# Side-by-side key-value products for batch 0 of an attention and highway kernel, and a new order of its steps

## The chip, the core and the metric

The kernel runs on one core of a Trainium2 chip. A core has five engines that run side by side, each through its own queue and in the order of that queue: TensorE (PE in the profile, with PEld for its weight loads), VectorE (DVE), ScalarE (ACT), GpSimd (POOL) and SyncE (SP), which here only issues DMAs. Engines wait for each other by semaphores. TensorE writes to PSUM; VectorE and ScalarE read it, GpSimd works on SBUF alone. The metric is the device time of one execution in microseconds.

## The reference

Eight batches, eight heads, 576 positions, 64 values a head. First an attention without a score matrix, then a highway layer:

```python
q_s = exp(q);  q_s = q_s / sum(q_s, over the head's 64 values)
k_s = exp(k);  k_s = k_s / sum(k_s, over the 576 positions)
kv  = einsum('bhsd,bhse->bhde', k_s, v)           # 64 x 64 for each batch and head
x   = einsum('bhsd,bhde->bhse', q_s, kv)          # then (4608, 512): all heads of a position in a row
H   = maximum(x @ w_h, 0)
T   = sigmoid(x @ w_t + b_t)
out = T * H + (1 - T) * x
```

Inputs and output are float32 in the chip's main memory: q, k and v 9.4 MB each, the output 9.4 MB.

## The kernel before, in words

Positions are put on partitions: 64 rows of 9 positions, for two heads at once, so that a [128, 4, 9 x 64] tile holds a batch (4 pairs of heads, called chunks). The work is cut into 36 tiles of 128 positions, nine for each pair of batches (tile 8, 17, ... holds the ninth positions of both batches). All of it is written as short steps with names, and the string `ORDER` (lines 16 to 63) lists some 710 of them. A loop at the end (lines 502 to 505) runs through that list and issues each step's instructions. Nothing is rescheduled, so the list sets the order of every engine's queue, and of SP's DMA queue too. A name has a batch or tile and a part; a letter behind a colon picks the engine (A ScalarE, D VectorE, P GpSimd, F a whole step at once).

The steps, in the order in which one tile needs them:

- `k`, `v`, `q`, `w`: loads of the inputs and the two weights (SP). `st`: stores of the output (SP). A tile of q, k or v has three buffers. Batches 0 to 2 load k and v in pieces (`load_kv`, line 181).
- `ek`: exp of k on ScalarE (line 252). `vc`: cast of v to half precision on any engine (258), into a tile that has a column of ones behind each 64 values.
- `kv`: for each position j, head of a pair and row half, one matmul of ek (stationary) with v and its ones (264), so that 65 columns hold kv and the sum of the exponentials. The accumulator `ps` has a PSUM bank for each row half. Batches 0 to 2 do it in two steps, chunks 0 and 1 (`kv_b_0`: k and v chunks 0, 1) and chunks 2 and 3 (`kv_b_1`); the others in one. `kr` takes the reciprocal of the sums (280) and `kn` multiplies with it into `kvb` (285), both on VectorE.
- `eq`: exp of q on ScalarE (295). `qt`: its transposes on TensorE (313). `qc`: their copy to SBUF (331). For batch 7 a DMA transposes (`qd`, 339).
- `xu`: q times kv and, by a column of ones, q's sum (350). `rs`, `x`: the division, on VectorE (369, 374). `xt`: transposes of x (381). `xe`: their copy (389), on VectorE or ScalarE.
- `bw`: the bias of the gate into its accumulator (396), by a ScalarE copy or a matmul; the gate has two banks. `mt`: the gate's four products (408). `mh`: those of the other branch (416).
- `th`: tanh in place of the sigmoid (430). `dd`: the maximum, on VectorE (439). `uu`: (tanh + 1) times it, on VectorE in one instruction or, with P, on GpSimd in two (443). `oo`: plus x (464).
- `whd`, `whc`, `wtc`: the weights' adjustment (the identity is taken from w_h) and cast. `bp`, `bc`, `bsplit`: the bias spread over 128 rows. `fill_n`: n matmuls of a blank tile into a spare bank (166), whose results nobody reads.

Some tiles (0, 4, 5, 6, 7) do xu to mh in two halves, each with one part of the heads; the last tile does its gate in two pieces of columns.

Of the kernel before, what the change touches and what calls it, by code (L numbers as in the profile page):

```python
# [26 lines left out]
xe_4_0:D xe_4_1:D mh_5_0 dd_5 mt_5_0 th_5_0 uu_5_0:P k_2_0 ek_2_1 bw_8:A ek_2_2 xu_6_0 rs_6_0 x_6_0 mt_4_1 xt_8_0
xe_8_0:D xu_6_1 rs_6_1 qt_2_0 x_6_1 xu_7_0 rs_7_0 x_7_0 mt_4_0 xt_6_0 xu_7_1 rs_7_1 xt_6_1 xe_6_0:D xe_6_1:D x_7_1
mt_8_0 ek_2_0 v_2_0 vc_2_0:D qc_2_0 mh_4_1 mh_4_0 xt_7_0 dd_4 xt_7_1 th_4_0 vc_2_1 kv_2_0 v_2_2 vc_2_3 vc_2_2:A kv_2_1
kr_2_1 mh_8_0 bw_6:A mh_6_1 th_8_0 mt_6_1 kr_2_0 oo_5_0 kn_2_1 uu_4_0:P kn_2_0 xu_9_0 dd_8 q_2_4 eq_2_2 eq_2_1 xe_7_1  # L30
uu_8_0:P oo_4_0 rs_9_0 x_9_0 mt_6_0 xe_7_0 qt_2_1 qc_2_1 th_6_0 mh_6_0 dd_6 mh_7_1 xt_9_0 xu_12_0 rs_12_0 x_12_0
uu_6_0:P oo_8_0 oo_6_0 xe_9_0:D mh_7_0 dd_7 bw_7:A mt_7_1 mt_7_0 xu_10_0 xt_12_0 mh_9_0 xe_12_0:D rs_10_0 q_3_0 x_10_0
eq_3_0 eq_3_1 qt_3_2 qc_3_2 dd_9 mh_12_0 xt_10_0 xe_10_0:D qt_3_1 qc_3_1 k_3_0 th_7_0 bw_10:A v_3_0 vc_3_0 xu_11_0
rs_11_0 bw_9:A mt_9_0 ek_3_0 ek_3_2 dd_12 vc_3_2:A x_11_0 qt_3_0 th_9_0 qc_3_0 uu_7_0:P oo_7_0 uu_9_0 mt_10_0 th_10_0
bw_12:A kv_3_0 qt_2_2 q_4_0 qc_2_2:A mh_10_0 eq_4_0:F kr_3_0 kn_3_0 xt_11_0 xe_11_0:D mt_12_0 dd_10 uu_10_0:P oo_9_0
oo_10_0 xu_14_0 rs_14_0 x_14_0 th_12_0 uu_12_0 oo_12_0 mh_11_0 qt_4_0 bw_11:A xu_13_0 rs_13_0 x_13_0 v_4_0 vc_4_0
xt_14_0 xe_14_0:D vc_4_2:A bw_14:A mt_11_0 th_11_0 xu_17_0 rs_17_0 x_17_0 qc_4_0:A xt_13_0 mh_14_0 dd_11 uu_11_0:P
oo_11_0 xu_15_0 rs_15_0 xe_13_0:D x_15_0 mt_14_0 dd_14 mh_13_0 xu_16_0 rs_16_0 x_16_0 bw_13:A xt_17_0 xe_17_0:D
mt_13_0 dd_13 k_4_0 ek_4_0 ek_4_2 q_4_9 kv_4_0 kr_4_0 kn_4_0 th_14_0 uu_14_0:P bw_17:A th_13_0 uu_13_0 xt_15_0 xe_15_0
qt_4_1 qc_4_1 mt_17_0 xu_18_0 rs_18_0 x_18_0 oo_14_0 q_5_0 eq_5_0 oo_13_0 v_5_0 vc_5_0 bw_15:A vc_5_2 mh_17_0 xt_16_0  # L40
xe_16_0:D dd_17 eq_4_2 eq_5_1 mt_15_0 th_15_0 xu_20_0 qt_4_2 k_5_0 rs_20_0 x_20_0 mh_15_0 th_17_0 uu_17_0:P oo_17_0
xt_18_0 mh_16_0 xu_19_0 dd_15 qc_4_2 xe_18_0:D rs_19_0 qt_5_0 qc_5_0 bw_16:A ek_5_0:F xt_20_0 x_19_0 q_6_0 xe_20_0:D
mt_16_0 th_16_0 bw_18:A qt_5_1 kv_5_0 eq_6_0:F dd_16 kr_5_0 kn_5_0 uu_16_0 bw_20:A xt_19_0 mh_18_0 qc_5_1:A st_1_0
st_1_1 mh_20_0 st_3_0 uu_15_0:P oo_15_0 xe_19_0:D xu_21_0 rs_21_0 x_21_0 oo_16_0 mt_18_0 th_18_0 k_6_0 st_3_1 v_6_0
mt_20_0 xu_22_0 dd_18 uu_18_0 oo_18_0 st_5_0 st_7_1 q_5_9 st_5_1 xt_21_0 rs_22_0 x_22_0 th_20_0 dd_20 uu_20_0:P
xe_21_0:D st_7_0 qt_6_0 mh_19_0 xu_23_0 rs_23_0 x_23_0 vc_6_2 dd_19 bw_19:A bw_21:A mt_19_0 ek_6_0 ek_6_2 mh_21_0
dd_21 xt_22_0 xe_22_0 xu_24_0 mt_21_0 mh_22_0 xt_23_0 rs_24_0 qc_6_0 x_24_0 vc_6_0:A kv_6_0 qt_6_1 th_19_0 uu_19_0:P
oo_20_0 q_6_9 dd_22 xe_23_0:D mh_23_0 kr_6_0 th_21_0 uu_21_0 oo_19_0 kn_6_0 bw_22:A mt_22_0 qc_6_1:A dd_23 xu_25_0
rs_25_0 x_25_0 eq_5_2 xt_24_0 qt_5_2 bw_23:A mt_23_0 th_22_0 oo_21_0 uu_22_0:P oo_22_0 qc_5_2:A xu_26_0 xe_24_0
rs_26_0 x_26_0 bw_24:A th_23_0 uu_23_0 xt_25_0 mh_24_0 dd_24 st_10_1 q_7_0 oo_23_0 v_7_0 st_10_0 vc_7_0 vc_7_2 k_7_0  # L50
mt_24_0 xe_25_0 eq_6_2 xu_27_0 qt_6_2 xt_26_0 mh_25_0 rs_27_0 x_27_0 xe_26_0:D xu_29_0 rs_29_0 bw_25:A mt_25_0 st_17_0
eq_7_0:F qd_7_0 qc_6_2:A dd_25 th_24_0 qd_7_1 x_29_0 xt_27_0 xe_27_0 uu_24_0 oo_24_0 mh_26_0 dd_26 xu_30_0 rs_30_0
th_25_0 x_30_0 st_12_0 uu_25_0:P mh_27_0 bw_27:A mt_27_0 st_14_1 dd_27 xt_30_0 xu_28_0 rs_28_0 q_7_9 st_12_1 bw_26:A
mt_26_0 st_14_0 st_23_0 st_16_0 st_16_1 xe_30_0:D mh_30_0 ek_7_0 oo_25_0 x_28_0 xt_28_0 xe_28_0:D ek_7_2 kv_7_0
xt_29_0 th_26_0 uu_26_0 oo_26_0 th_27_0 uu_27_0:P mh_28_0 bw_30:A mt_30_0 kr_7_0 kn_7_0 xu_31_0 st_21_0 bw_28:A
mt_28_0 dd_30 xe_29_0:D rs_31_0 dd_28 th_30_0 uu_30_0:P mh_29_0 x_31_0 xt_31_0 xe_31_0:D oo_27_0 oo_30_0 bw_29:A
xu_33_0 eq_7_2 th_28_0 rs_33_0 uu_28_0 mt_29_0 qt_7_2 bw_31:A mh_31_0 x_33_0 xt_33_0 xu_32_0 th_29_0 dd_29 rs_32_0
uu_29_0 qc_7_2:A oo_29_0 x_32_0 xe_33_0 mt_31_0 mh_33_0 xt_32_0 bw_33:A th_31_0 dd_31 st_8_0 st_19_0 st_26_0 xu_34_0
xe_32_0 uu_31_0 rs_34_0 mt_33_0 x_34_0 oo_28_0 st_28_0 st_30_0 oo_31_0 st_31_0 st_25_0 mh_32_0 xu_35_0 dd_33 xt_34_0
bw_32:A mt_32_0 th_33_0 uu_33_0:P oo_33_0 dd_32 xe_34_0:D mh_34_0 rs_35_0 x_35_0 xt_35_0 bw_34:A th_32_0 uu_32_0 dd_34  # L60
xe_35_0 mt_34_0 th_34_0 uu_34_0 oo_32_0 st_33_0 st_32_0 oo_34_0 st_34_0 bw_35_0 mh_35_0 dd_35 mt_35_0 th_35_0 uu_35_0
# [5 lines left out]
def kernel(  # L67
# [49 lines left out]
    spare = turned.rearrange("p a c d -> p (a c d)").bitcast(FP32)
    T = {}
# [142 lines left out]
        copy(v16[b % NV][:, c:c + n, :, 0:D], T[f"v32{b}"][:, c:c + n].rearrange("p c (j d) -> p c j d", j=NJ))  # L261


    def kv(e, b, k):
        ps = once(f"kvps{b}", lambda: ps_x.tile([P, 2, DM], FP32, tag="xu", name=f"kv_{b}"))
        for kk in range(*halves(b, k)):
            for j in range(NJ):
                for hh in range(2):
                    for w in range(2):
                        rows, cols = slice(64 * hh, 64 * hh + 64), slice(64 * w, 64 * w + 64)  # L270
                        nc.tensor.matmul(  # L271
                            ps[cols, hh, 65 * kk:65 * kk + 65], T[f"ek{b}"][rows, j, 2 * kk + w],
                            v16[b % NV][rows, 2 * kk + w, j, 0:65],
                            start=(j == 0), stop=(j == NJ - 1), skip_group_check=True)
# [261 lines left out]
```

## Time and profile before

| | |
|---|---|
| median of 3 runs | 117.8 us (117.66 to 118.46) |
| the profiled execution | 117.78 us |
| its span | 116.0 us |
| TensorE busy | 109.2 us, 1355 matmuls |
| VectorE, ScalarE, GpSimd busy | 93.7, 91.2, 90.9 us |
| moved by DMA | 40.58 MB, mean 350 GB/s |
| mean granted TensorE clock | 0.99 |

The span reaches from the first to the last event that the profile has of the core; 1.78 us of the profiled execution lie outside it. A group of instructions goes by its line in the code. The slices cut the span into 40 parts of 2.9 us and give each engine's busy share in tenths. Matmul ends are modelled, so a busy TensorE is not always a TensorE at its peak. The chain is followed back from the last instruction, at each step to what released it. Times in the views count from the span's start.

### The profile page before, as it was taken

How to read it: one execution, taken by the hardware profiler on the slowest of the kernel's cores; microseconds unless marked ns; L12 is line 12 of the kernel's file. 1: busy time of each engine (PE TensorE's matmuls, PEld its weight loads, DVE VectorE, ACT ScalarE, POOL GpSimd, SP SyncE). 2: the span in 40 equal slices, each digit the busy share in tenths (PEclk: the TensorE clock that was granted, in tenths of full speed). 3: DMA queues.
4: the chain of work that ended last, by engine and by line, in shares of the span. 5: the costliest groups of instructions: out<-in, count | busy, mean ns of one | idle time of the engine just before them, and what ended most of it. 6: DMA issues, size and time to landing. Idle time of an engine off the chain costs nothing.

```text
span 116.0 us, 3454 instructions
## 1 busy us (share of the span) xinstructions
PE 109.2 (94%) x1355; PEld 62.8 (54%) x1355; DVE 93.7 (81%) x231; ACT 91.2 (79%) x139; POOL 90.9 (78%) x103
## 2 busy tenths in 40 slices
PE   5999999999999999999999999999999999999930
...
PEclk9999999999999999999999999999999999999995
DMA  2999999999999999999999999999999999894965
GB/s 49 375 397 379 407 391 378 390 377 367 384 384 379 390 393 366 367 393 355 349 386 388 363 401 406 391 384 332 370 398 376 148 276 394 343 364 166 401 257 181
DMA packets 24755, 40.58 MB, mean 350 GB/s; under 512 B 5410, under 2 KB 12834, under 8 KB 24740
## 3 DMA queue, kind: packets, MB, share of 16 engines
...
q10 hardware_dynamic: 148, 0.14, 0.4%
...
## 4 chain that ended last, share of the span: by engine, by line
PE 54%; POOL 26%; DVE 6%; issue 6%; DMA 2%; ACT 1%; POOLq 1%; ACTq 0%
POOL o L473 14%; PE gps L421 14%; PE tps L413 13%; PE turned L168 10%; POOL u L453 6%; PE kv L271 4%; PE xu L363 4%; PE turned L386 4%; PE qps L326 3%; POOL g L452 3%; DMA out_dram<-o 2%; POOL v L261 2%; DVE x L378 2%; DVE d L441 2%; DVE xT L393 1%
## 5 line engine op out<-in xcount | busy, mean ns | idle before, releaser
L473 POOL TENSOR_TENSOR o<-u,x 128x512 f32<-128x512 f16 (+1 forms) x36 | 40.5, 1142 | 2.1 <-DVE u L455 1.2
L413 PE MATMUL tps<-w16t,xT 128*128 128x512 f16 (+1 forms) x148 | 37.2, 373 | 0.0
L421 PE MATMUL gps<-w16h,xT 128*128 128x512 f16 x144 | 36.9, 379 | 0.0
L378 DVE TENSOR_TENSOR x<-xu,rs 128x512 f16<-128x512 f32 (+1 forms) x41 | 25.5, 624 | 2.5 <-POOL g L452 0.5
L441 DVE SCALAR_TENSOR_TENSOR d<-x,gps 128x512 f16<-128x512 f16 x36 | 24.1, 677 | 0.5 <-PE gps L421 0.4
L453 POOL TENSOR_TENSOR u<-g,d 128x512 f16<-128x512 f16 x19 | 21.9, 1155 | 1.6
L261 POOL CAST v<-v 128x576 f16<-128x576 f32 (+1 forms) x14 | 12.6, 906 | 11.4 <-DMA v<-in_v_dram 11.3
L255 ACT ACTIVATE ek<-k 128x576 f16<-128x576 f32 (+2 forms) x21 | 18.8, 930 | 2.6 <-DMA k<-in_k_dram 2.5
L413 PEld LDWEIGHTS <-xT 128*128 128x128 f16 x148 | 13.4, 98 | 10.7 <-ACT xT L393 0.2
L421 PEld LDWEIGHTS <-xT 128*128 128x128 f16 x144 | 12.9, 98 | 10.9 <-DVE xT L393 0.8
L401 ACT COPY tps<-ball 128x512 f32<-128x512 f32 x29 | 16.8, 590 | 2.4 <-DVE u L455 2.1
L363 PE MATMUL xu<-kvb,eq 128*128 128x130 f16 (+1 forms) x160 | 15.4, 225 | 0.3 <-DVE x L378 0.2
L363 PEld LDWEIGHTS <-eq 128*128 128x128 f16 (+1 forms) x160 | 10.4, 100 | 8.4 <-DVE x L378 3.6
L386 PE MATMUL turned<-idh,x 128*128 128x128 f16 x144 | 14.5, 220 | 0.1
L309 ACT ACTIVATE qe<-q 128x1024 f16<-128x1024 f32 (+2 forms) x11 | 9.5, 896 | 5.3 <-DMA q<-in_q_dram 5.3
L386 PEld LDWEIGHTS <-x 128*128 128x128 f16 x144 | 10.2, 98 | 6.1 <-DVE x L378 1.6
L455 DVE SCALAR_TENSOR_TENSOR u<-tps,d 128x512 f16<-128x512 f32 (+1 forms) x17 | 11.4, 668 | 2.5 <-ACT tps L437 1.9
L168 PE MATMUL turned<-blank 128*128 128x512 f16 x45 | 12.1, 420 | 1.3 <-POOL blank L150 1.3
L452 POOL TENSOR_SCALAR g<-th 128x512 f16<-128x512 f16 x19 | 11.7, 618 | 1.2 <-DVE x L378 1.2
L435 ACT ACTIVATE th<-tps 128x512 f16<-128x512 f32 x19 | 11.2, 592 | 1.7 <-PE tps L413 1.6
L393 DVE COPY xT<-turned 128x512 f16<-128x512 f16 (+1 forms) x28 | 10.6, 384 | 2.3 <-PE turned L386 2.3
L437 ACT ACTIVATE tps<-tps 128x512 f32<-128x512 f32 (+1 forms) x18 | 10.0, 556 | 2.4 <-PE tps L413 2.4
...
## 6 DMA issues: line engine op xcount, KB each, us to landing
...
```

The source lines that it names most:

```text
L168: nc.tensor.matmul(spare, blank[:, 0:P], blank, start=True, stop=True, skip_group_check=True)
L255: nc.scalar.activation(t[:, :, c:c + n].rearrange("p j c d -> p c j d"), T[f"k32{b}"][:, c:c + n].rearrange("p c (j d) -> p c j d", j=NJ), ...
L363: nc.tensor.matmul(dst, turned_q(b, jp, n), kvb[b % NKV][:, hh, kk], start=True, stop=True, skip_group_check=True)
L378: nc.vector.tensor_mul(t[:, k0:k1], sums(i, k)[:, :, :, 0:64], T[f"rs{i}_{k}"][:, 0:k1 - k0].unsqueeze(3).to_broadcast([P, k1 - k0, 4, D]))
L386: nc.tensor.matmul(t[:, n], T[f"x{i}"][:, n0 + n % 2:n0 + 2 * P:2], idh, is_transpose=True, start=True, stop=True, skip_group_check=True)
L401: nc.scalar.copy(t[:, cs], ball[:, cs])
L413: nc.tensor.matmul(T[gate(i, k)][:, cs], T[f"xT{i}"][:, n], w16["t"][:, n, cs], start=False, stop=(n == parts[-1] and not first), skip_gro ...
L421: nc.tensor.matmul(t, T[f"xT{i}"][:, n], w16["h"][:, n], start=(first and n == parts[0]), stop=(n == parts[-1] and not (first and len(part ...
L441: nc.vector.scalar_tensor_tensor(t, T[f"x{i}"], -0.5, T[f"gps{i}"], op0=ALU.mult, op1=ALU.max)
L452: nc.gpsimd.tensor_scalar(g, T[f"th{i}"], 1.0, 1.0, op0=ALU.add, op1=ALU.mult)
L453: nc.gpsimd.tensor_mul(t, g, T[f"d{i}"])
L473: eng.tensor_add(t[:, cs], T[f"u{i}_{h}"][:, cs], T[f"x{i}"][:, cs])
```

## The change

Two things change. For batches in `BROAD`, which is batch 0 alone, one matmul of `kv` takes the exponentials of the keys of both heads of a chunk side by side as its stationary block (64 rows, 128 columns in place of 64), and v with its ones of both heads as its moving one (130 columns in place of 65). Its result has the products of each head's keys with each head's values, and `kr` and `kn` read those of a head with itself; the others are left unread. The 72 matmuls of batch 0 become 36. And the list of steps is written anew:

```diff
+    BROAD = (0,)
+
     def kv(e, b, k):
         ps = once(f"kvps{b}", lambda: ps_x.tile([P, 2, DM], FP32, tag="xu", name=f"kv_{b}"))
         for kk in range(*halves(b, k)):
             for j in range(NJ):
                 for hh in range(2):
+                    if b in BROAD:
+                        rows, heads_ = slice(64 * hh, 64 * hh + 64), slice(2 * kk, 2 * kk + 2)
+                        nc.tensor.matmul(
+                            ps[:, hh, 130 * kk:130 * kk + 130],
+                            T[f"ek{b}"][rows, j, heads_].rearrange("p c d -> p (c d)"), v16[b % NV][rows, heads_, j, 0:65],
+                            start=(j == 0), stop=(j == NJ - 1), skip_group_check=True)
+                        continue
                     for w in range(2):
...
     def kv_of(b, k):
         k0, k1 = halves(b, k)
-        return T[f"kvps{b}"][:, :, 0:130].rearrange("p h (k e) -> p h k e", k=2)[:, :, k0:k1]
+        n = 2 if b in BROAD else 1
+        return T[f"kvps{b}"][:, :, 0:130 * n].rearrange("p h (k w e) -> p h k w e", k=2, w=n)[:, :, k0:k1]
...
-        rz = T[f"rz{b}_{k}"] = dp.tile([P, 2, 2], FP32, tag="rz", name=f"rz_{b}_{k}")
-        nc.vector.reciprocal(rz[:, :, 0:k1 - k0], kv_of(b, k)[:, :, :, 64])
+        n = 2 if b in BROAD else 1
+        rz = T[f"rz{b}_{k}"] = dp.tile([P, 2, k1 - k0, n], FP32, tag="rz", name=f"rz_{b}_{k}")
+        nc.vector.reciprocal(rz, kv_of(b, k)[:, :, :, :, 64])
...
-            r, e0 = slice(64 * w, 64 * w + 64), 65 * w
+            r, e0, n = slice(64 * w, 64 * w + 64), 65 * w, w if b in BROAD else 0
             nc.vector.tensor_mul(
-                kvb[b % NKV][r, :, k0:k1, e0:e0 + 64], kv_of(b, k)[r, :, :, 0:64],
-                T[f"rz{b}_{k}"][r, :, 0:k1 - k0].unsqueeze(3).to_broadcast([64, 2, k1 - k0, 64]))
+                kvb[b % NKV][r, :, k0:k1, e0:e0 + 64], kv_of(b, k)[r, :, :, n, 0:64],
+                T[f"rz{b}_{k}"][r, :, :, n].unsqueeze(3).to_broadcast([64, 2, k1 - k0, 64]))
```

The beginning of the list, old and new:

```diff
-setuppool q_0_0 v_0_0 fill_8 fill_8 b_32 b_0 eq_0_0 k_0_0 ek_0_0 qt_0_0 setupdve bsplit bp bc fill_8 ek_0_1 vc_0_0:D
-v_0_1 vc_0_1 kv_0_0 kr_0_0 k_0_2 fill_8 ek_0_3 v_0_2 v_0_3 vc_0_2 qc_0_0 kn_0_0 xu_0_0 vc_0_3 ek_0_2 kv_0_1 kr_0_1
-kn_0_1 q_0_4 fill_5 eq_0_1 eq_0_2 xu_1_0 rs_1_0 rs_0_0 x_1_0 x_0_0 fill_8 xt_1_0 xe_1_0:D qt_0_1 w_h_0 whd_1:P whd_0:P
-whc_0:A qc_0_1 xt_0_0 xu_0_1 rs_0_1 x_0_1 bw_1 xe_0_0 xu_3_0 rs_3_0 x_3_0 qt_0_2 bw_0 w_h_2 whd_2:P whd_3:P whc_2:A
-w_t_2 wtc_2:P xt_0_1 mh_0_0 xe_0_1:D xu_2_0 xt_3_0 xe_3_0 rs_2_0 w_t_0 wtc_0:P mh_1_0 q_1_0 mh_0_1 qc_0_2:A x_2_0
-xt_2_0 dd_1 dd_0 k_1_2 eq_1_0 v_1_2 mt_1_0 th_1_0 uu_1_0 vc_1_3 oo_1_0 ek_1_2 ek_1_3 xe_2_0:D mt_0_1 mt_0_0 th_0_0
-qt_1_0 qc_1_0 mh_3_0 bw_2 mt_2_0 vc_1_2:A kv_1_1 uu_0_0 oo_0_0 th_2_0 bw_3 mt_3_0 k_1_0 ek_1_1 ek_1_0 dd_3 kr_1_1
-v_1_0 vc_1_0 vc_1_1:A kn_1_1 xu_5_1 th_3_0 rs_5_1 x_5_1 mh_2_0 dd_2 uu_2_0:P uu_3_0:P oo_2_0 oo_3_0 xt_5_1 xu_4_1
-kv_1_0 kr_1_0 rs_4_1 bw_5 kn_1_0 xe_5_1 mt_5_1 x_4_1 q_1_4 eq_1_2 xu_5_0 rs_5_0 qt_1_2 qc_1_2 bw_4 xu_4_0 xu_8_0 x_5_0
+setuppool fill_8 b_0 fill_8 b_32 setupdve bsplit bp fill_8 fill_8 q_0_0 w_h_0 v_0_2 vc_0_2:D whd_1:P eq_0_0 qt_0_0
+k_0_2 whd_0:P whc_0:A v_0_3 vc_0_3:A ek_0_3 ek_0_2 kv_0_1 kr_0_1 fill_8 v_0_1 k_0_0 ek_0_1 qc_0_0 kn_0_1 xu_0_1 rs_0_1
+x_0_1 v_0_0 vc_0_1 ek_0_0 vc_0_0:A kv_0_0 q_0_4 eq_0_2 eq_0_1 fill_6 kr_0_0 kn_0_0 xu_0_0 xt_0_1 rs_0_0 x_0_0 xu_1_0
+rs_1_0 xe_0_1 x_1_0 qt_0_1 xt_0_0 qc_0_1 bc bw_0 bw_2 xe_0_0 xt_1_0 w_h_2 whd_2:P mh_0_0 whd_3:P whc_2:A xu_2_0
+xe_1_0:D rs_2_0 x_2_0 mh_0_1 dd_0 mh_1_0 w_t_2 wtc_2:P w_t_0 wtc_0:P xt_2_0 xe_2_0 qt_0_2 xu_3_0 rs_3_0 mt_0_1 mt_0_0
+mh_2_0 k_1_2 ek_1_2 th_0_0 dd_1 x_3_0 mt_2_0 ek_1_3 v_1_2 vc_1_2:A vc_1_3:D uu_0_0:P oo_0_0 q_1_0 dd_2 xt_3_0 xe_3_0:D
+th_2_0 uu_2_0 oo_2_0 qc_0_2 bw_1 mt_1_0 kv_1_1 bw_3 kr_1_1 kn_1_1 eq_1_0 qt_1_0 qc_1_0 k_1_0 mh_3_0 ek_1_0 ek_1_1
+xu_5_1 rs_5_1 x_5_1 v_1_0 vc_1_0:A th_1_0 mt_3_0 th_3_0 dd_3 xt_5_1 vc_1_1 kv_1_0 xe_5_1:D kr_1_0 xu_4_1 rs_4_1 bw_5
+kn_1_0 uu_1_0:P mt_5_1 x_4_1 bw_4 q_1_4 uu_3_0:P oo_1_0 oo_3_0 eq_1_2 qt_1_2 qc_1_2 xu_5_0 rs_5_0 x_5_0 eq_1_1 xu_4_0
 ...
```

The rest of the list holds the same steps, with these that matter at the end. The last loads ahead of batch 7's `qd` were q_7_0, v_7_0, st_10_0, k_7_0 (q_7_9 came later, behind the `qd`); they are q_7_0, q_7_9, st_7_1, st_10_0, k_7_0, v_7_0. From `kv_7_0` on TensorE did `xt_29 mh_28 mt_30 xu_31 mt_28 mh_29 xt_31 xu_33 mt_29 qt_7_2 mh_31 ...`; now it does `xt_29 mh_30 mt_30 xu_31 mt_29 mh_29 xu_33 xt_31 mh_28 mt_28 xu_32 ...`, with qt_7_2 ahead of kv_7_0. The cast vc_7_2 goes from GpSimd to ScalarE. In all, `vc` has 9 steps on ScalarE in place of 6, 11 on GpSimd in place of 14 and 2 on VectorE as before; `qc` 5 on ScalarE in place of 9 and 17 on VectorE in place of 13; `xe` 12 on ScalarE in place of 13 and 29 on VectorE in place of 28. `uu` keeps 19 tiles on GpSimd, seven of them others than before. The fills number 46 in place of 45.

More of the change, by code (lines that the diff above doesn't have):

```diff
@@ L22 @@
-xt_2_0 dd_1 dd_0 k_1_2 eq_1_0 v_1_2 mt_1_0 th_1_0 uu_1_0 vc_1_3 oo_1_0 ek_1_2 ek_1_3 xe_2_0:D mt_0_1 mt_0_0 th_0_0
-qt_1_0 qc_1_0 mh_3_0 bw_2 mt_2_0 vc_1_2:A kv_1_1 uu_0_0 oo_0_0 th_2_0 bw_3 mt_3_0 k_1_0 ek_1_1 ek_1_0 dd_3 kr_1_1
-v_1_0 vc_1_0 vc_1_1:A kn_1_1 xu_5_1 th_3_0 rs_5_1 x_5_1 mh_2_0 dd_2 uu_2_0:P uu_3_0:P oo_2_0 oo_3_0 xt_5_1 xu_4_1
-kv_1_0 kr_1_0 rs_4_1 bw_5 kn_1_0 xe_5_1 mt_5_1 x_4_1 q_1_4 eq_1_2 xu_5_0 rs_5_0 qt_1_2 qc_1_2 bw_4 xu_4_0 xu_8_0 x_5_0
-eq_1_1 xt_5_0 qt_1_1 rs_4_0 x_4_0 mh_5_1 q_2_0 eq_2_0 k_2_2 rs_8_0 xe_5_0:D qc_1_1:A x_8_0 ek_2_3 xt_4_0 xt_4_1
@@ L27 @@
[L27 to L61, printed above, removed]
@@ L62 @@
-oo_35_0 bw_35_1 mt_35_1 st_35_0 th_35_1 uu_35_1 oo_35_1:D st_35_1:A
+setuppool fill_8 b_0 fill_8 b_32 setupdve bsplit bp fill_8 fill_8 q_0_0 w_h_0 v_0_2 vc_0_2:D whd_1:P eq_0_0 qt_0_0
+k_0_2 whd_0:P whc_0:A v_0_3 vc_0_3:A ek_0_3 ek_0_2 kv_0_1 kr_0_1 fill_8 v_0_1 k_0_0 ek_0_1 qc_0_0 kn_0_1 xu_0_1 rs_0_1
+x_0_1 v_0_0 vc_0_1 ek_0_0 vc_0_0:A kv_0_0 q_0_4 eq_0_2 eq_0_1 fill_6 kr_0_0 kn_0_0 xu_0_0 xt_0_1 rs_0_0 x_0_0 xu_1_0
+rs_1_0 xe_0_1 x_1_0 qt_0_1 xt_0_0 qc_0_1 bc bw_0 bw_2 xe_0_0 xt_1_0 w_h_2 whd_2:P mh_0_0 whd_3:P whc_2:A xu_2_0
@@ new lines @@
+rs_4_0 xu_8_0 rs_8_0 x_4_0 qt_1_1 q_2_0 eq_2_0 qc_1_1:A xt_5_0 xe_5_0:D x_8_0 k_2_0 ek_2_1 ek_2_0 mh_5_1 xt_4_0 xt_4_1
+xe_4_1:D mh_5_0 xe_4_0:D dd_5 mt_5_0 th_5_0 xt_8_0 xu_6_1 rs_6_1 x_6_1 mt_4_1 xu_6_0 k_2_2 v_2_2 vc_2_2 ek_2_2 vc_2_3
+mt_4_0 th_4_0 bw_8:A rs_6_0 x_6_0 xu_7_0 ek_2_3 rs_7_0 x_7_0 xe_8_0:D qt_2_0 mh_4_1 mh_4_0 qc_2_0 xt_6_1 xt_6_0 xu_7_1
+xe_6_1:D rs_7_1 xe_6_0:D mt_8_0 xt_7_0 kv_2_1 v_2_0 vc_2_0 vc_2_1:A kv_2_0 dd_4 x_7_1 xt_7_1 uu_5_0:P kr_2_0 oo_5_0
+uu_4_0:P oo_4_0 kr_2_1 kn_2_0 kn_2_1 mh_8_0 dd_8 bw_6:A mt_6_1 xe_7_0:D mt_6_0 xu_9_0 rs_9_0 x_9_0 mh_6_1 xe_7_1 q_2_4
@@ new lines @@
+eq_2_2 eq_2_1 qt_2_1 qc_2_1 th_8_0 mh_6_0 dd_6 th_6_0 xt_9_0 xe_9_0:D bw_7:A mh_7_1 mt_7_1 xu_12_0 mt_7_0 mh_9_0
+qt_2_2 rs_12_0 x_12_0 xu_10_0 q_3_0 uu_6_0 uu_8_0:P eq_3_0:F oo_8_0 th_7_0 rs_10_0 x_10_0 xt_12_0 xe_12_0:D mh_7_0
+dd_7 qc_2_2:A qt_3_0 qc_3_0 bw_9:A mt_9_0 xt_10_0 xu_11_0 rs_11_0 x_11_0 xe_10_0:D oo_6_0 k_3_0 ek_3_0:F dd_9 mh_12_0
+v_3_0 qt_3_1 bw_12:A mt_12_0 qc_3_1 dd_12 xt_11_0 vc_3_0:A vc_3_2 kv_3_0 kr_3_0 th_9_0 uu_7_0:P oo_7_0 uu_9_0:P oo_9_0
+xe_11_0:D kn_3_0 th_12_0 qt_3_2 qc_3_2 bw_11:A uu_12_0 oo_12_0 mh_10_0 mh_11_0 q_4_0 eq_4_0 eq_4_1 bw_10:A xu_14_0
@@ new lines @@
+mt_11_0 th_11_0 qt_4_0 qc_4_0:A rs_14_0 x_14_0 dd_10 xu_13_0 rs_13_0 x_13_0 xt_14_0 dd_11 mt_10_0 xe_14_0 k_4_0
+xu_17_0 rs_17_0 x_17_0 qt_4_1 v_4_0 vc_4_0 xt_13_0 xe_13_0:D mh_14_0 th_10_0 ek_4_0 uu_10_0 oo_10_0 dd_14 q_4_9 q_5_0
+k_5_0 vc_4_2 st_1_1 v_5_0 st_3_0 q_6_9 st_5_1 st_3_1 xu_15_0 rs_15_0 x_15_0 st_1_0 xt_17_0 mh_13_0 bw_13:A bw_14:A
+mt_14_0 xe_17_0 ek_4_2 th_14_0 k_6_0 q_5_9 v_6_0 st_5_0 dd_13 xu_16_0 rs_16_0 x_16_0 xt_15_0 mt_13_0 th_13_0 xe_15_0:D
+bw_17:A kv_4_0 qc_4_1 uu_11_0:P oo_11_0 eq_5_0:F uu_14_0 uu_13_0:P oo_14_0 kr_4_0 kn_4_0 oo_13_0 bw_15:A xt_16_0
@@ new lines @@
+xe_16_0:D mh_17_0 dd_17 mt_17_0 xu_18_0 rs_18_0 x_18_0 th_17_0 uu_17_0 vc_5_2 oo_17_0 mh_15_0 mt_15_0 xt_18_0 xu_20_0
+rs_20_0 dd_15 x_20_0 mh_16_0 dd_16 ek_5_0 bw_16:A mt_16_0 xu_19_0 rs_19_0 x_19_0 qt_5_1 qc_5_1 th_15_0 uu_15_0:P
+xe_18_0 bw_18:A ek_5_2 eq_4_2 mt_18_0 xu_21_0 mh_18_0 rs_21_0 x_21_0 qt_5_0 dd_18 xt_20_0 xe_20_0:D q_6_0 vc_5_0:A
+kv_5_0 th_18_0 uu_18_0 th_16_0 oo_15_0 oo_18_0 uu_16_0:P oo_16_0 xt_19_0 xe_19_0:D mh_20_0 st_10_1 xt_21_0 st_7_0
+q_7_0 q_7_9 bw_20:A mt_20_0 st_7_1 st_10_0 k_7_0 vc_6_2 kr_5_0 kn_5_0 xe_21_0:D qc_5_0:A xu_22_0 rs_22_0 dd_20 x_22_0
@@ new lines @@
+mh_21_0 bw_19:A mt_19_0 ek_6_0 ek_6_2 th_20_0 bw_21:A xt_22_0 xe_22_0 th_19_0 vc_6_0:A uu_20_0:P dd_21 xu_23_0 rs_23_0
+x_23_0 mh_19_0 dd_19 mt_21_0 th_21_0 xu_24_0 qt_4_2 xt_23_0 rs_24_0 x_24_0 qc_4_2 eq_5_2 xe_23_0 uu_19_0:P oo_20_0
+mh_22_0 oo_19_0 uu_21_0 oo_21_0 kv_6_0 kr_6_0 kn_6_0 bw_22:A qt_5_2 qc_5_2 dd_22 mh_23_0 dd_23 eq_6_2 bw_23:A mt_22_0
+eq_6_0:F xu_25_0 rs_25_0 qt_6_2 th_22_0 uu_22_0:P oo_22_0 bw_24:A qc_6_2 x_25_0 mt_23_0 xt_24_0 xe_24_0:D qt_6_0
+xu_26_0 qc_6_0:A rs_26_0 x_26_0 xt_25_0 xe_25_0:D mt_24_0 qt_6_1 qc_6_1 xu_27_0 rs_27_0 xt_26_0 th_23_0 uu_23_0:P
@@ new lines @@
+oo_23_0 xe_26_0:D bw_25:A th_24_0 eq_7_2 mh_24_0 eq_7_0:F v_7_0 qd_7_0 qd_7_1 x_27_0 mt_25_0 dd_24 uu_24_0 oo_24_0
+vc_7_0 xu_30_0 mh_26_0 rs_30_0 x_30_0 xt_27_0 xe_27_0:D st_14_1 mh_25_0 xu_28_0 dd_26 th_25_0 rs_28_0 xt_30_0 dd_25
+uu_25_0:P oo_25_0 x_28_0 bw_27:A mt_27_0 st_19_0 st_12_0 st_12_1 st_14_0 st_8_0 st_23_0 xe_30_0:D bw_26:A mt_26_0
+xu_29_0 rs_29_0 x_29_0 qt_7_2 xt_28_0 xe_28_0:D mh_27_0 dd_27 ek_7_0 ek_7_2 vc_7_2:A th_26_0 uu_26_0 kv_7_0 kr_7_0
+st_16_0 kn_7_0 oo_26_0 st_26_0 st_17_0 th_27_0 uu_27_0:P oo_27_0 xt_29_0 qc_7_2 mh_30_0 dd_30 bw_30:A mt_30_0 bw_29:A
```

7 lines of the change are left out of this document (added).

## The prediction

> **What bounds the kernel now.** I read the page's slices first, then the busy times by stage, then the chain that ended last, and at the end the order of time around the places where the steps move.
>
> ```profile
> PE   5999999999999999999999999999999999999930
> ...
> PEclk9999999999999999999999999999999999999995
> DMA  2999999999999999999999999999999999894965
> GB/s 49 375 397 379 407 391 378 390 377 367 384 384 379 390 393 366 367 393 355 349 386 388 363 401 406 391 384 332 370 398 376 148 276 394 343 364 166 401 257 181
> ```
>
> A slice is 2.9 us. TensorE is full in all but the first and the last two, at full clock, and the DMA engines are full until 90 us. Two resources are tight at once. But a filled PE row proves nothing by itself, since matmul ends are modelled and 45 of them (L168) multiply zeros. So I split the span where the last prologue stall ends:
>
> ```profile
> 0.00:18.00 18.00, 16.39 (x161) 8.16 (x161) 10.11 (x37) 9.08 (x12) 5.63 (x17) 1.00 0.91 334
> 18.00:111.30 93.30, 92.81 (x1194) 54.61 (x1194) 82.41 (x192) 81.81 (x127) 84.06 (x86) 1.00 1.03 362
> 111.30:116.00 4.70, 0.00 (x0) 0.00 (x0) 1.19 (x3) 0.31 (x1) 1.24 (x2) 0.75 0.51 180
> ```
>
> (columns: length, then busy us of PE, PEld, DVE, ACT, POOL, then clock, DMA share, GB/s.) To check the middle row I priced PE by starts: in the chain four 512-column matmuls take 0.86 us (0.2157 each), four turned blocks 0.22, four xu 0.23, a whole kv 0.71 to 0.77. Laid against the starts of PE's rows in order of time, the work explains all of 18 to 111 us but some 2.6 us of small gaps (the largest 0.36, ahead of kv_6 at 79.36). **The bound** is therefore 16 to 18 us of prologue, 93 us of TensorE with almost no holes, and a 4.7 us tail. The chain does run through POOL from 51 to 76 us, but PE is full beside it.
>
> Beside it stands the DMA bound. The last loads are v and k of batch 7; k waits twelve us in its queue and ends just in time:
>
> ```profile
> 79.77 0.59 SPq L184 DMA_DIRECT2D k<-in_k_dram  x1
> ...
> 91.85 2.22 ACT L255 ACTIVATE ek<-k 128x1152 f16<-128x1152 f32 x2 [0.64 <-DMA k<-in_k_dram]
> ...
> 94.25 0.78 PE L271 MATMUL kv<-v,ek 64*64 64x65 f16 x72
> ```
>
> ACT idled 0.64 us for k, and kv_7 starts 0.18 us after the exponentials end. From there PE is full to its last matmul at 111.2.
>
> **The broad matmuls.** Batch 0's two kv steps become 18 matmuls each in place of 36. The old price:
>
> ```profile
> 9.05 0.41 PE kv L271 x36
> ...
> 11.41 0.60 PE kv L271 x35
> 12.01 1.19 PE turned L168 x5
> 13.20 0.23 PE xu L363 x4
> 13.43 1.73 PE turned L168 x8
> ```
>
> So 0.41 us, 11.4 ns an instruction (0.60 is the one that waited for a cast). No row shows a 64x128 block with 130 columns. The nearest is xu: 128x128, 130 columns, 0.058 us. If the two row halves cannot overlap, 18 x 0.058 = 1.05 us; if they run side by side, 0.52; if the cost follows the instruction count, 18 x 0.0114 = 0.21. I take 0.52, because the old row already shows blocks side by side (36 x 65 columns one after another would be some 1.0 us). That is +0.1 us a step, with ends of -0.2 and +0.64. Both stand in the prologue, where a fill of 8 (1.73 us) or 6 (1.3 us) follows and kr and kn run meanwhile; only the second, ahead of xu_0_0, is on the path: +0.1. kr reads 4 instead of 2 sums a row (181 against 166 ns by the two rz rows); kn is unchanged in size (289 ns each).
>
> [...]
>
> **The prologue made anew.** SP's queue now has w_h_0 (512 KB) second, and q_1_0 behind k_1_2 and v_1_2. Ahead of the last of batch 0's k and v stood 2816 KB; now 3328 KB. 0.52 MB at the 379 to 407 GB/s of these slices is 1.3 us. In bytes, k_0_2 lands at about 8.3, v_0_3 at 9.1, k_0_0 at 11.4, v_0_0 at 12.2 us (q_0_4, w_h_2, w_t_2 and w_t_0 keep their cumulative bytes, so their times: 12.6 to 19.1).
>
> On ACT the cast vc_0_3 stands ahead of both first exponentials and waits for v_0_3: 9.1 + 0.67 + 2 x 0.63 = 11.0 for kv_0_1, against 8.98 for the first kv of before. Then ek_0_1, ek_0_0 and vc_0_0 from 11.4: 11.4 + 1.26 + 0.67 = 13.4 for the second kv, against 11.34. Then the fill of 6, kr and kn (0.17 + 0.58): xu_0_0 at 15.6, xu_1_0 at 15.9 against 13.04. So attention starts 2 to 3 us later. What takes most of that back is slack that before spent on zeros (1.73 us of fill at 13.43) and on the wait for the weights: x_1_0 ends near 17.4, mh_0_0 stands at 17.6 (before 17.3), qc_0_1 is followed by xu_2_0 at 18.1, whc_2 ends at about 17.9 to 18.3 and releases mh_0_1, mh_1_0 ends 19.6, and the first mt comes at 20.2 as before, since w_t_0 still lands at 19.1 and its POOL cast takes 1.04.
>
> From there I went on by hand in queue order. At the end of mt_1_0 the new order has done what before has done at 24.48 us, where it enters kv_1_1, but for qt_1_0 (0.45): so before stands there at 24.03, after at 24.1. Then three small new waits on PE, each with all later PE work queued behind it: bw_3 for the gate bank that DVE's uu_2_0 frees (0.2), qt_1_0 for eq_1_0, whose q now lands at about 23.5 behind k_1_2 and v_1_2 (hidden by the first), and xu_5_1 for qc_1_0, which sits behind uu_2_0, qc_0_2, kr and kn on DVE (0.3). vc_1_0 is ACT's now and behind v_1_0 at 26.6; kv_1_0 comes at 27.7, and with xu_4_1 (0.12), which before had already done, the kernel is **0.5 us behind** at 28 us. qt_1_1, at 30.4 in before, gives the same 0.5.
>
> **The middle.** The counts of each kind times their rows: POOL loses 3 casts (2 x 0.67 + 1.15 = 2.5 us of 90.9); ACT gains these 2.5 and gives back 4 short qc (1.5), a half xe (0.37) and some 0.2 by a merged exponential, +0.4 of 91.2; DVE takes 4 short qc (1.14) and a half xe (0.27), +1.4 of 93.7. PE does the same work but for kv. No engine comes near PE's 93 of 93.3 in this stretch. I compared how much PE work stands between a producer and its reader: the shortest xu to xt distances after batch 1 are 1.2 to 1.4 us before and 1.3 to 1.5 after, xt to its first product 0.97 both. So I cost the middle at **0**: at best it could win back part of the 2.6 us of gaps, at worst add as much. Its cover is PE's own full queue.
>
> **The end.** After kv_7 the new order has mh_30 more and qt_7_2 less, so PE needs 0.86 - 0.11 = 0.75 us more from kv_7 to its end, and kv_7 must start at 93.5 to keep 111.2. Now v_7 is loaded last, and q_7_9 (128 KB, 0.33 us) stands ahead of it; the stores ahead are ten in both. So v_7 lands at 91.85 + 0.33 = 92.2, its two casts (POOL 1.15 beside ACT 1.15, with th_26, th_27 and bw_30 queued behind ACT's) end at 93.4, and kv_7 starts at 93.45: 111.45 at the end, +0.25. This is a gate and not a term to add: with 0.5 us from the prologue PE is there at 94.0. The tail's gate, product and stores have the same shapes: 0.
>
> **Sum**: 0.5 (prologue, the broad matmul's 0.1 in it) + 0 + 0. The profiled execution took 117.78 us, its span 116.0 and 1.78 around it; it lies on the median of 117.8. 117.78 + 0.5 = **118.3 us**.
>
> **Rivals.** *Stays full, shifted* (my forecast, 117.2 to 119.0): 0.55.
>
> *The new order closes gaps*: POOL's relief lets the 2.6 us of holes shut. For it: the chain runs on POOL from 51 to 76. Against: PE is full there anyway, and the gate at 92.2 us is set by bytes, which do not change. Half of the holes and a faster stream give 117.8 - 1.3 = 116.5: 0.10.
>
> *ACT becomes the bound early* (slower): when PE has done 15.7 us of real work, ACT must have done 22.9 us in the new order, 18.5 in the old. It cannot start before 4.75, and by my run it waits some 5.5 us for v_0_3, k_0_0, q_0_4, whd_2 and xt_2 on the way: 33.2 against 29.7 for PE. What of these 3.5 us is for batch 2 (eq_2_0, ek_2) can come late. It decides at kv_1_0: if vc_1_0 ends after 28 us PE stands, from then on one for one. Half gives 118.3 + 1.3 = 119.6, all 121: 0.35.
>
> **Range**: 116.9 to 120.2 leaves most of the fast rival and the top third of the slow one out; kv's ends (-0.2, +0.5 on the path) lie inside. A change under 1% (1.2 us) can't be told from none here. Faster 0.10, same 0.55, slower 0.35.
>
> **What would show it.** Second kv near 13.4 us and 0.5 us long; first mt at 20.2; kv_1_0 near 28; PE holes after 18 us still near 3 us; kv_7 at 93.5 to 94.3 with DMA as its releaser. I am wrong if a kv of 18 takes over 1 us, if the loads behind w_h_0 land in another order of time than their bytes say, or if ACT's row shows PE waiting in 24 to 40 us.

## The result

| | before | after |
|---|---|---|
| median, us | 117.88 (117.66 to 118.46, 6 runs) | 119.69 (119.34 to 120.23, 6 runs) |
| profiled execution, us | 117.78 | 119.34 |
| its span, us | 116.0 | 117.6 |
| TensorE, VectorE, ScalarE, GpSimd busy, us | 109.2, 93.7, 91.2, 90.9 | 109.6, 95.1, 91.2, 88.8 |

The ratio is 1.0153, with a 95% interval of 1.0115 to 1.019: the changed kernel is slower by 1.8 us, by the interval 1.4 to 2.2. The forecast of 118.3 us was 1.4 us too low. The time lies in the range of 116.9 to 120.2, and near the 119.6 us of the rival in which ScalarE holds TensorE up early.

The slices of the page after, which stand against the row of nines of before:

```profile
PE   5999999999999689999999999999999999999930
...
ACT  4337763989995499998989999999999995665320
```

A slice is 2.94 us. TensorE, full from the second slice on in before, has a 6 and an 8 in the 14th and 15th slice, some 38 to 44 us. ScalarE has a 5 and a 4 in the 13th and 14th: it is not loaded in the place where TensorE runs dry, it is idle just ahead of it.

The same by stretches of time, for the kernel after (length, busy us of PE, PEld, DVE, ACT, POOL with their counts, then the clock, the DMA share and GB/s):

```profile
0.00:18.00 18.00, 16.56 (x119) 8.27 (x120) 8.67 (x33) 10.19 (x15) 5.25 (x16) 1.00 0.92 338
18.00:36.00 18.00, 17.87 (x211) 10.19 (x210) 16.04 (x48) 15.15 (x25) 12.56 (x15) 1.00 1.06 377
36.00:44.00 8.00, 6.45 (x117) 3.81 (x116) 5.86 (x18) 5.18 (x9) 7.59 (x9) 1.00 1.05 389
44.00:111.30 67.30, 67.28 (x868) 39.72 (x867) 62.08 (x136) 59.87 (x88) 61.48 (x61) 1.00 0.99 340
```

and the third of these stretches for the kernel before:

```profile
36.00:44.00 8.00, 8.00 (x129) 4.93 (x128) 7.52 (x19) 7.69 (x14) 7.67 (x9) 1.00 1.06 390
```

In these 8 us TensorE is idle for 1.55 us more than before, VectorE for 1.7, ScalarE for 2.5. Nothing else in the middle is like it. The timeline of the kernel after shows what they wait for (start, length, engine, line, operation, count, and in brackets the idle time before it and who ended it):

```profile
36.47 0.58 ACT L412 COPY tps<-ball 128x512 f32<-128x512 f32 x1
...
37.66 1.20 DVE L300 TENSOR_TENSOR kvb<-kv,rz 64x128 f16<-64x128 f32 x4
...
38.90 0.69 DVE L452 SCALAR_TENSOR_TENSOR d<-x,gps 128x512 f16<-128x512 f16 x1
...
39.41 0.59 PE L432 MATMUL gps<-w16h,xT 128*128 128x512 f16 x2
39.50 0.28 DVE L404 COPY xT<-turned 128x256 f16<-128x256 f16 x1
...
39.87 0.37 ACT L404 COPY xT<-turned 128x256 f16<-128x256 f16 x1 [2.82 <-DVE xT L404]
...
40.14 1.36 ACT L320 ACTIVATE qe<-q 128x256 f16<-128x256 f32 x2
...
41.56 0.62 PE L337 MATMUL qps<-idh,qe 128*128 128x128 f16 x8 [1.55 <-ACT qe L320]
```

Read it from the bottom. TensorE is at `qt_2_1` and waits 1.55 us for the exponentials `eq_2_2` and `eq_2_1`. ScalarE has nothing to do from 37.1 us on (run 1 below shows that the q they read is there at 37.8), but ahead of them in its queue stands `xe_7_1`, the copy of one half of tile 7's transposes, and that one waits 2.82 us for `xe_7_0`, the copy of the other half of the same tile. The new list writes `xe_7_0:D`, so that half is VectorE's, and there it stands behind four `kn` and a `dd`. In the code both halves write one tile, and the one that comes second in the list waits for the first, 2.82 us here; runs 2 and 4 below test that it is the place in the list that decides. In before both halves were ScalarE's, and behind the exponentials:

```profile
37.73 1.36 ACT L309 ACTIVATE qe<-q 128x256 f16<-128x256 f32 x2
39.01 0.63 ACT L393 COPY xT<-turned 128x256 f16<-128x256 f16 x2
```

To see how much of the loss this is, I laid the priced TensorE work against the starts once more, as in the prediction, and with equal price for both forms of `kv`, so that the broad form, and the one fill more, count as lateness. The new order is behind the old one by 0.48 us at `kv_2` (36.6 us), 1.94 at `qt_2_1`, 1.90 at `kv_3`, 1.54 at `kv_7` and 1.49 at the end. The two spans differ by 1.6. So the sum is 0.5 in the prologue, 1.5 at one place, and 0.4 to 0.5 won back in the 50 us behind it.

### The profile page after: what moved, and what is told of

Its sections match the earlier page's. It is cut to its first block, busy times and chain, and to the rows that moved or that the text cites. A ratio compares the mean times of both kernels' runs of the same rounds, so it can differ in the third digit from the quotient of the medians.

```text
span 117.6 us, 3383 instructions
## 1 busy us (share of the span) xinstructions
PE 109.6 (93%) x1320; PEld 62.9 (54%) x1320; DVE 95.1 (81%) x236; ACT 91.2 (78%) x136; POOL 88.8 (76%) x100
## 4 chain that ended last, share of the span: by engine, by line
PE 86%; DVE 7%; ACT 2%; POOL 1%; issue 1%; DVEq 0%; ACTq 0%; POOLq 0%
PE tps L424 24%; PE gps L432 24%; PE turned L168 10%; PE xu L374 8%; PE turned L397 7%; PE kv L280 5%; PE qps L337 4%; PE qps L332 2%; DVE u L466 1%; DVE kvb L300 1%; DVE x L389 1%; DVE d L452 1%; ACT qe L320 1%; PE kv L273 1%; POOL o L484 1%
## 5 line engine op out<-in xcount | busy, mean ns | idle before, releaser
L168 PE MATMUL turned<-blank 128*128 128x512 f16 x46 | 12.6, 432 | 1.3 <-POOL blank L150 1.3
L261 POOL CAST v<-v 128x1152 f16<-128x1152 f32 (+1 forms) x11 | 10.1, 926 | 4.8 <-DMA v<-in_v_dram 4.0
L383 DVE RECIPROCAL rs<-xu 128x8 f32<-128x8 f32 (+1 forms) x41 | 8.0, 198 | 4.4 <-PE xu L374 3.6
```

Of the source, the lines that this page charges most:

```text
L168: nc.tensor.matmul(spare, blank[:, 0:P], blank, start=True, stop=True, skip_group_check=True)
```

## The experiments

**Theory**: the wait of one half copy for the other costs the 1.5 us, and it is a matter of place in the list, not of ScalarE's load. **Rival**: ScalarE is short of time early, so whatever is moved ahead makes something else late. A second question is what the broad products cost by themselves.

**1. The exponentials ahead of the half copy**, in the kernel after:

```diff
-... dd_8 bw_6:A mt_6_1 xe_7_0:D mt_6_0 xu_9_0 rs_9_0 x_9_0 mh_6_1 xe_7_1 q_2_4
-eq_2_2 eq_2_1 qt_2_1 ...
+... dd_8 bw_6:A q_2_4 eq_2_2 eq_2_1 mt_6_1 xe_7_0:D mt_6_0 xu_9_0 rs_9_0 x_9_0 mh_6_1 xe_7_1
+qt_2_1 ...
```

> The changed kernel, with the two exponentials of batch 2's q (eq_2_2, eq_2_1) put ahead of the copy xe_7_1 in ScalarE's queue; nothing else moves. Theory W (the wait): the copy stands 2.8 us in that queue for VectorE's xe_7_0, the exponentials behind it, and TensorE stands 1.7 us at qt_2_1 for them; so without it TensorE has no hole over 0.4 us near 40 us and the median is 119.7 - 1.5 = 118.2 us, +0.3 % on the kernel before, which is what the later start of batch 1 leaves. Theory K (the broad matmuls are what costs): 119.5 or more. Theory P (the new order is tight all over, the next wait takes the hole over): 119.0 to 119.5, with a new hole of a microsecond further on.

118.77 us (118.5 to 119.04), a ratio to before of 1.0068, with its 95% interval [1.0047, 1.0089]; the other runs are given in the same way. The time is 0.6 us over theory W's 118.2 and under theory P's 119.0. The timeline of this kernel:

```profile
37.77 1.36 ACT L320 ACTIVATE qe<-q 128x256 f16<-128x256 f32 x2 [0.34 <-DMA q<-in_q_dram]
...
40.55 0.61 PE L337 MATMUL qps<-idh,qe 128*128 128x128 f16 x8
40.58 0.37 ACT L404 COPY xT<-turned 128x256 f16<-128x256 f16 x1 [1.44 <-DVE xT L404]
```

`qt_2_1` starts with no wait. ScalarE still idles 1.44 us for VectorE's half, now with nothing urgent behind it. The wait is gone, and what is left of the loss, 0.7 us, is not far from the 0.5 us of the prologue; the last section says what else is in it.

**2 and 3. The two halves in the other order**, one name moved, profiled first and then timed:

```diff
-... dd_8 bw_6:A mt_6_1 xe_7_0:D mt_6_0 xu_9_0 rs_9_0 x_9_0 mh_6_1 xe_7_1 q_2_4
+... dd_8 bw_6:A xe_7_1 mt_6_1 xe_7_0:D mt_6_0 xu_9_0 rs_9_0 x_9_0 mh_6_1 q_2_4
```

> The changed kernel, with xe_7_1 listed ahead of xe_7_0 (ScalarE's and VectorE's own orders stay as they are, xe_7_1 still ahead of the exponentials). It tells what ScalarE waits for. If it is the other half of the same tile, written just ahead of it in the list: ScalarE runs the copy as soon as xt_7_1 is done (near 37.6 us), the exponentials end near 39.4, the hole at qt_2_1 is gone, and the time is 118.2. If it is something else that VectorE does in between (kn_2, dd_8): the hole of 1.7 us and 119.5 to 119.7 stay.

> The changed kernel with xe_7_1 listed ahead of xe_7_0 once more, now timed. Theory W: 1.5 us less than the changed kernel, 118.0 to 118.3, a ratio of 1.000 to 1.004. The first profiles point to a second thing: the first 16 fills took 5.1 to 6.4 us by when the clock rose, and in the new list 32 fills stand ahead of batch 0's first products, so runs should spread by up to 0.8 us: 117.7 where the clock rises by 5.3 us, 118.5 where it rises after 6.3.

117.69 us in the profiled execution of run 2; timed in run 3, 118.2 (117.97 to 118.49), 0.9984 [0.997, 0.9999]. The timeline of run 2:

```profile
37.64 0.37 ACT L404 COPY xT<-turned 128x256 f16<-128x256 f16 x1 [0.39 <-PE turned L397]
...
37.91 1.36 ACT L320 ACTIVATE qe<-q 128x256 f16<-128x256 f32 x2
...
39.83 0.61 PE L337 MATMUL qps<-idh,qe 128*128 128x128 f16 x8
```

ScalarE's copy now waits for the transposes alone. The same copies run on the same engines with the same lengths; one name has changed its place, and the kernel is level with before instead of 1.5% slower. ScalarE's busy time is not less (91.4 us against 91.2). The rival falls, and the wait is worth 1.6 to 1.7% (1.0153, or in run 7 1.0144, against 0.9984, each beside before on its own chip); the profiled executions, 119.34 and 117.69 us, differ by 1.65 us.

**4. The wait put into the kernel before**: its two half copies of tile 7 placed as after has them, one on VectorE, behind `dd_8`, and both ahead of the exponentials.

```diff
-... xu_9_0 dd_8 q_2_4 eq_2_2 eq_2_1 xe_7_1
-uu_8_0:P oo_4_0 rs_9_0 x_9_0 mt_6_0 xe_7_0 qt_2_1 ...
+... xu_9_0 dd_8 xe_7_0:D xe_7_1 q_2_4 eq_2_2 eq_2_1
+uu_8_0:P oo_4_0 rs_9_0 x_9_0 mt_6_0 qt_2_1 ...
```

> The kernel before, into whose list the same wait is put: the copy xe_7_0 goes to VectorE behind dd_8, and xe_7_1 and then xe... of ScalarE stands behind it in the list, ahead of batch 2's two q exponentials (eq_2_2, eq_2_1); nothing else moves. Theory W: dd_8 ends at 39.4 us in before, xe_7_0 at 39.75, xe_7_1 at 40.15, eq_2_1 at 41.5, so qt_2_1 starts at 41.55 in place of 39.62 and TensorE stands 1.7 to 1.9 us: 119.3 to 119.7, a ratio of 1.012 to 1.016. Theory G (what ends batch 7's loads holds the end, an earlier hole is made up): 118.0 to 118.4.

119.61 us (119.51 to 119.92), 1.011 [1.0085, 1.0135]. Its timeline has the same picture:

```profile
40.33 0.37 ACT L393 COPY xT<-turned 128x256 f16<-128x256 f16 x1 [2.08 <-DVE xT L393]
...
42.01 0.62 PE L326 MATMUL qps<-idh,qe 128*128 128x128 f16 x8 [1.65 <-ACT qe L309]
```

The time is in theory W's range, the ratio just under it. So these two names alone cost the old order 1.3 us: the wait is sufficient in either order.

**5. The broad products alone**: before's list, with `BROAD = (0,)` and the code that goes with it.

```diff
+    BROAD = (0,)
```

> The kernel before with its own list of steps, and batch 0's products by 36 broad matmuls. Theory W: each step costs 0.62 us in place of 0.41, most of it beside fills and kr and kn; 117.9 + 0.1 = 118.0, a ratio of 1.000 to 1.003. Theory K: at least 1 % over the kernel before.

118.67 us (117.67 to 119.04), 1.0038 [1.0013, 1.0064]. The ratio is just over theory W's range and far under theory K's 1%. The runs fall in two groups: three at 117.67 to 117.81, nine at 118.48 to 119.04. In the first the broad form costs nothing, in the second 0.4 to 0.6 us, against runs of before whose clock rose at the same moment; the last section tells the groups apart.

**6. The new order with the old products**: `BROAD = ()` in the kernel after.

```diff
-    BROAD = (0,)
+    BROAD = ()
```

> The changed list of steps with the old 72 narrow matmuls for batch 0. Theory W: the two steps give back 0.2 us each, of which the second is on the way to xu_0_0: 119.5, a ratio of 1.012 to 1.016 against the kernel before; the hole at qt_2_1 stays at 1.5 us or more. Theory K: 118.2 or less.

119.4 us (119.25 to 119.75), 1.0121 [1.0099, 1.0143]. The wait at `qt_2_1` stays (1.68 us of hole). The order alone makes the kernel slower; 0.3 to 0.4 us may be the products', but the intervals overlap and do not separate them.

**7. The kernel after once more**, unchanged, beside runs of before on another chip.

> The changed kernel itself once more, as the measure for the others of this chip: a ratio of 1.012 to 1.019, the hole at qt_2_1 of 1.5 to 2 us in its trace wherever the clock rises.

119.92 us (119.84 to 120.18), 1.0144 [1.0112, 1.0177], with the same hole of 1.55 us: the result repeats.

**8 and 9. Fewer fills.** Runs 1 and 5 pointed at the blank products at the start, so I took four away, in the kernel of run 3 and in the kernel before:

```diff
-setuppool fill_8 b_0 fill_8 b_32 setupdve bsplit bp fill_8 fill_8 q_0_0 ...
+setuppool fill_8 b_0 fill_8 b_32 setupdve bsplit bp fill_8 fill_4 q_0_0 ...
```
```diff
-... eq_0_0 k_0_0 ek_0_0 qt_0_0 setupdve bsplit bp bc fill_8 ek_0_1 vc_0_0:D
+... eq_0_0 k_0_0 ek_0_0 qt_0_0 setupdve bsplit bp bc fill_4 ek_0_1 vc_0_0:D
```

> As e2, and the last fill of 8 ahead of batch 0's first transposes is one of 4 (0.86 us less of TensorE's queue). If a late rise of the clock costs time because the fills then end after ScalarE's exponentials (10.9 us) and hold kv_0_1, the late runs come down: 117.6 to 117.9 in all, 0.3 us or more under e2's median. If the fills are not on the path, the same as e2. If the pause makes the clock fall back, 1 us or more over e2.

> The kernel before with a fill of 4 in place of 8 behind batch 0's first transposes, nothing else. There kv_0_0 waits for an exponential that ends at 9.0 us, and the fill ends at 8.95 when the clock rises at 4.4 us, later by half of each us that it rises later. If a late rise costs the kernel before too: its slow runs (118.4 to 118.8) come down, a ratio of 0.996 to 0.998. If not: 1.000.

With the half copy moved: 117.9 us (117.72 to 118.21), 0.9967 [0.9952, 0.9982]. Before with four fewer: 117.99 (117.8 to 118.2), 0.9977 [0.9958, 0.9995]. Both gain some 0.2% (run 8 against run 3, run 9 against before), and the spread of before (117.77 to 118.83 beside it) more than halves. In the chain of the first of the two, the start of batch 0 no longer hangs on the fills but on the load of `v_0_3`, its cast and the two exponentials:

```profile
2.73 6.54 DMA v<-in_v_dram
...
9.29 0.67 ACT v L261
9.96 1.17 ACT ek L255 x2
...
11.18 0.69 PE kv L273 x18
```

**10. The old place of `w_h_0`**: run 3's kernel, with the load of `w_h_0` and the steps on it behind `q_0_4` again, and six fills fewer.

```diff
-... fill_8 fill_8 q_0_0 w_h_0 v_0_2 vc_0_2:D whd_1:P eq_0_0 qt_0_0
-k_0_2 whd_0:P whc_0:A v_0_3 ... q_0_4 eq_0_2 ... qc_0_1 bc bw_0
+... fill_8 fill_2 q_0_0 v_0_2 vc_0_2:D eq_0_0 qt_0_0
+k_0_2 v_0_3 ... q_0_4 w_h_0 whd_1:P whd_0:P eq_0_2 ... qc_0_1 whc_0:A bc bw_0
```

> As e2, with w_h_0 loaded behind q_0_4 as in the kernel before (its adjustment and cast moved behind the q exponentials), and 6 fills fewer ahead of batch 0's first transposes, since k and v then come 1.3 us sooner. If the later k and v of batch 0 are what costs the 0.5 us ahead of 28 us: 0.3 to 0.5 us under e9, 117.3 to 117.6, under the kernel before. If the wait for w_t_0 (its cast ends near 18.9) sets the first gate product anyway: within 0.2 us of e9.

117.77 us (117.53 to 118.11), 0.9953 [0.9937, 0.9969]: the fastest of all, faster than both kernels. `kv` starts at 9.73 in place of 11.18 us, but the first `mt` only at 19.61 in place of 20.31, with a hole of 0.76 us ahead of `bw_2`, whose bias copy now stands behind `whc_0` on ScalarE. Of 1.45 us won at the front 0.7 are left at the first `mt`, and some 0.13 in the medians of the two kernels. That is the second case of the expectation, a wait for the weights: in this run and in run 11 the second half of the first gate product comes 0.2 us late, and run 11's timeline names GpSimd's cast of w_t for it.

**11 and 12. The old products in the kernels of 10 and 8** (`BROAD = ()`, nothing else).

> As e7, with the narrow matmuls back in batch 0 (72 in place of 36). With the fills trimmed the two kv steps start when ScalarE is done, so their 0.2 us each is on the way to xu_1_0; but w_t_0's cast still ends near 18.9 us. If the broad matmuls cost what their rows say and nothing hides it: 0.2 to 0.4 us under e7, a ratio of 0.992 to 0.994. If the wait for the weights hides it: within 0.15 us of e7.

> The kernel with the half copy moved up and four fills fewer, but batch 0's key-value products again as 72 matmuls of 65 columns. In the profile of its broad sibling TensorE waits 1.27 us for the exponentials ahead of the first key-value step at 11.18 us and is then full from 11.18 to beyond 21 us, with each broad step 0.62 us long against 0.41 to 0.43 for a narrow one. Theory 1, the broad form's price is on TensorE's path once that first wait is over: two steps of 0.2 us less put the first gate product 0.4 us earlier (19.9 in place of 20.3), and the median is 0.3 to 0.45 us under the sibling's, a ratio to the kernel before of 0.993 to 0.9945 (sibling 0.9967). Theory 2, the price is hidden here, by the weights' wait behind it or by the wait for v_7 at the end: ratio 0.9955 to 0.998, and the profile shows a new hole ahead of the first products or ahead of kv_7 near 93.5 us.

118.13 us (118.03 to 118.38), 0.9999 [0.9982, 1.0016], and 118.21 us (118.01 to 118.49), 0.9993 [0.9977, 1.0009]. Both expectations had some 0.4 us less than with the broad form, or about the same; both kernels came out 0.3 to 0.4 us higher, which was in neither. The kernels of a pair ran on different chips, each beside before: by their ratios runs 10 and 11 are 0.5% apart, with intervals that do not meet, and runs 8 and 12 are 0.3% apart, with intervals that touch. The prologue does what was expected: in run 12 `kv` takes 0.41 us and the first `mt` starts at 19.94 in place of 20.31. But at `kv_1_0` the two are level (27.64 and 27.66 us), and at the end the narrow kernels meet the gate that the prediction had put at 93.45 us. Run 12's timeline:

```profile
88.53 4.01 SPq L353 DMA_TRANSPOSE eq<-qe  x2
...
92.73 1.15 ACT L261 CAST v<-v 128x1152 f16<-128x1152 f32 x1 [0.45 <-DMA v<-in_v_dram]
92.83 1.14 POOL L261 CAST v<-v 128x1152 f16<-128x1152 f32 x1 [1.34 <-PE turned L397]
...
94.02 0.92 PE L280 MATMUL kv<-v,ek 64*64 64x65 f16 x72 [0.34 <-POOL v L261]
```

and that of its broad sibling, run 8:

```profile
88.34 2.84 SPq L353 DMA_TRANSPOSE eq<-qe  x2
...
91.49 1.15 POOL L261 CAST v<-v 128x1152 f16<-128x1152 f32 x1
...
93.49 0.89 PE L280 MATMUL kv<-v,ek 64*64 64x65 f16 x72
```

The last load, v_7, lands about a microsecond later; the two DMA transposes issued while it is under way take 4.0 us in place of 2.8, in run 11 4.3 in place of run 10's 3.0. Up to `kv_6` the kernels of each pair are within 0.2 us of each other, at `kv_7` 0.5 us apart, so in these profiled executions the late load makes most of the difference. Run 12's is the slowest of its twelve (118.49 us, the median 118.21); run 11's lies on its median. Why loads issued within 0.3 us of each other end so differently stays open: the transposes and the load overlap in all four, and no run moved the one away from the other.

## Why the prediction was right or wrong

**The prologue, 0.5 us: right, with one term mis-sized.** The new order is 0.48 us behind at 36.6 us. The points of the run by hand held: second `kv` at 13.87 (13.4 forecast), `xu_0_0` at 15.73 (15.6), first `mt` at 20.36 (20.2), `kv_1_0` at 27.71 (27.7). The reason given for the first `kv` was half the truth. Loads and casts would have released it at 11.18, as run 8 shows; in the kernel after TensorE comes to it only at 11.30, held by fills and `qt_0_0`, as its chain shows:

```profile
1.32 5.65 PE turned L168 x16
...
7.40 3.45 PE turned L168 x16
10.85 0.45 PE qps L337 x8
11.30 0.62 PE kv L273 x18
...
13.87 0.62 PE kv L273 x18
```

The prediction had not counted the fills as a wait at all.

**The broad matmul: 0.62 us a step, not 0.52**, 34 ns each, between the ends 0.21 and 1.05. Added to TensorE are 0.21 us a step and not 0.1. What arrives of it depends on what ends last: nothing to 0.6 us in before's order (run 5), and in runs 11 and 12 the kernels with the old form are even the slower ones, by a late load whose cause is open. The 18 matmuls of a 64x128 block with 130 columns take 0.62 us in after and in run 5; the 36 of a 64x64 block with 65 columns, in whose place they stand, take 0.41 in before's first step and again in run 6.

**The middle, 0 us: wrong, and this is the step that failed.** It rested on two checks: that no engine is busy for as much as TensorE, and that TensorE has as much work between an `xu` and its `xt`, and between an `xt` and its product, as before. Neither asks what is queued behind an instruction that waits. The prediction counted that "a half xe" moves to VectorE (0.27 us) and ScalarE gives back 0.37; it priced the copy and not its place, and put the middle at 0. The half that stays on ScalarE waits for the half that moved, and the exponentials that feed `qt_2_1` stand behind it: 1.5 us. The other term of the middle was not zero either: 0.4 to 0.5 us came back between 42 and 111 us. Run 2, which has no hole, wins back the same 0.4 us, so this belongs to the new order and is not a delay being made up. Part of it can be named: by starts and prices the gap ahead of `kv_6` shrinks from 0.36 us, which in before ended with VectorE's `x`, to 0.15, and the one ahead of `kv_4` from 0.27 to 0.17. GpSimd has 2.1 us less to do in the new order, which may have a part in it; no run tested it.

**The end, a gate at 93.45 us: it did not bind.** TensorE came to `kv_7` at 95.03, when both casts of v_7 had ended (the second at 94.67). In runs 11 and 12, with the losses ahead of it gone, the gate closes at 93.78 and 94.02, by the load that the prediction named; in runs 8 and 10, where v_7 was there sooner, `kv_7` starts at 93.49 and 93.28.

**The rivals.** "ACT becomes the bound early" gave 119.6 and the window of 24 to 40 us, and the prediction said that it would be wrong if ACT's row showed TensorE waiting there; the wait runs from 40.0 to 41.6, at the edge of that window. Engine and size agree, the size in part by luck: 119.6 stands for half of 2.7 us, and how the 3.5 us that the text adds up become 2.7 is not shown. Its mechanism was not right: it added up what ScalarE must have done, decided it at `vc_1_0`, and called the work for batch 2 free to come late. `kv_1_0` came on time, and it was batch 2's exponentials that came late, behind an idle ScalarE. "The order closes gaps" is there too, as the 0.4 to 0.5 us of the middle: the two signs stood in one kernel.

**The chances.** 0.55 for no change hung on the zero of the middle, the one term for which the prediction named ends as wide as the 2.6 us of holes and no instruction. The new order had moved almost every step; a walk through ScalarE's queue like the one done by hand up to 28 us, carried 12 us further, passes `xe_7_1`. That 119.69 us still lies inside the range is owed to the room kept for the slow rival; the sum had nothing for such a wait.
